# Weight slots, the last expert and the output blocks of a soft mixture of experts

## The chip, the cores and the metric

The program runs on one core of a Trainium2 chip. The metric is the time of one execution on the device, in microseconds; the lower the better. The core has TensorE (PE, with PEld for its weight loads), VectorE (DVE), ScalarE (ACT), GpSimd (POOL) and SyncE (SP), whose queue issues every DMA of this kernel; 16 DMA engines move the data.

## The reference

Attention, a gated MLP and a soft mixture of experts stand in a row; the change is in the last. All is fp32.

```python
x = attention(rmsnorm(q), rmsnorm(k), v)     # 4 batches, 12 heads, 448 tokens, 64 -> [1792, 768]
x = (silu(x @ w_gate) * (x @ w_val)) @ w_out # 768 -> 1536 -> 768
logits = x @ phi                             # [1792, 32]: 8 experts x 4 slots
d = softmax(logits, over tokens)
slot_input = (d.T @ x).reshape(8, 4, 768)
for e in range(8):
    slot_out[e] = relu(slot_input[e] @ w1[e]) @ w2[e]   # 768 -> 1024 -> 768
c = softmax(logits, over slots)
out = c @ slot_out                           # [1792, 768]
```

## The kernel before

Attention pairs of heads and the MLP's weight tiles run interleaved in an order written out by hand; the MLP's last batch ends at about 664 us of the span. The logits and the slot sums are gathered batch by batch; w_out is applied to the 32 slot sums only (`sip`), and so the experts see 32 rows.

The experts' weights (w1 and w2, 8 x 6 MB) come in 32 units of 1.5 MB (`eunits`), each loaded by `load_unit` into a slot of a ring of 15 (`unit_tile`, 12,288 bytes a partition): 11 slots on the right side of SBUF, free early, of which three first hold w_out, and NL = 4 in the pool `tail` on the left, which overlies the tiles of the MLP (raw, wh0, the x tiles, raw3, wh1, hT in this order) and so comes free as these are read for the last time. Unit u goes to slot (u + 3) % 15, and its load is issued behind the matmuls of unit u - 15. Units are (e, i, n): i = 0 is half of w1, by rows; i = 1 half of w2, by rows; i = 2 half of w2, by columns (pieces of 1,536 bytes, four DMAs of 384 KB). Experts 0 to 5 go by i = 0, 0, 1, 1. Experts 6 and 7 first do both halves of w1; then come the column halves n = 0 of both, then n = 1 of both.

For i = 0 the slot inputs `sit` are stationary (32 columns) and the weights move; four matmuls side by side in column groups fill `hacc`. ACT takes the relu, TensorE transposes, DVE puts the expert's four slots into the zeroed `h1m`. For i = 1 and 2 `h1m` is stationary, and all experts add up in one PSUM tile `so` (four column groups of 192 columns of the output).

The combine weights: `combine1` takes the softmax over slots; `combine2` (POOL) spreads a batch over the four row groups, `combine3` transposes it into `ct`, [128, 1792]: the weights of all tokens, once in each row group. Both run behind units 2 to 7, one batch a unit; `ct` has a tile of its own, the spread weights (`c3`) two.

The output: when n = 0 of experts 6 and 7 is done, `slot_out(0)` copies half of `so` to `sos`, and `output(0, i)` runs for 16 blocks of 112 tokens: two matmuls side by side in two row groups (stationary: 32 rows x 112 tokens of `ct`; moving: 192 columns of `sos`), a copy by DVE and one by ACT into a slot that is free again, and a DMA for one or two blocks. Then come the matmuls of the last two units, `slot_out(1)`, and 16 blocks of the other half. SP's queue issues all these DMAs in program order.

Of the kernel before, what the change touches and what calls it, by code (L numbers as in the profile page):

```python
# [21 lines left out]
def attn_moe_softmoe_kernel(  # L22
# [15 lines left out]
    nc = tc.nc  # L38
# [904 lines left out]
        nc.vector.reciprocal(out=cm, in_=cm)  # L943
        nc.vector.tensor_tensor(out=cv_, in0=cv_, in1=cmb, op=ALU.mult)

    def combine2(pool, b):

        c3s[b] = pool.tile([CP, NC, 4, NS], F32, tag="c3", name="c3", bufs=2)
        nc.gpsimd.tensor_copy(out=c3s[b], in_=ce[:, b].unsqueeze(2).to_broadcast([CP, NC, 4, NS]))

    def combine3(b, ct):

        c3 = c3s.pop(b)
        cp = pt_tile("cp")
        for c in range(NC):
            nc.tensor.transpose(
                cp[:, CP * c : CP * c + CP], c3[:, c].rearrange("p i s -> p (i s)"), ident[:CP, :CP]
            )
        nc.scalar.copy(out=ct[:, S * b : S * b + S], in_=cp[:, :S])


    KD2, KH2 = KD // 2, KH // 2


    eunits = [(e, i, n) for e in range(E - 2) for i in range(2) for n in range(2)]
    eunits += [(e, 0, n) for e in (E - 2, E - 1) for n in range(2)]
    eunits += [(e, 2, n) for n in range(2) for e in (E - 2, E - 1)]
    NE = len(eunits)

    NR, NL = (9, 2), 4  # L970
    NRT = sum(NR)
    wtile = {}
    wo = []
# [2 lines left out]
    def unit_tile(u):  # L976

        slot = (u + NG) % (NRT + NL)
        pool = pools[0 if slot < NR[0] else 1 if slot < NRT else 2]
        m = 2 if NRT <= slot < NRT + 2 or slot == NRT + 3 else 1  # L980
        t = [pool.tile([P, KD2 * F // m], F32, tag=f"w{slot}{i}", name="w") for i in range(m)]
        return t[0] if m == 1 else t

    def load_wo(g):
        t = unit_tile(g - NG).rearrange("p (j d) -> p j d", d=DM)
        for j in range(4):
            nc.sync.dma_start(out=t[:, j, :], in_=w32["o", 4 * g + j])
        wo.append(t)

    def load_unit(u):  # L990
        if u >= NE:
            return
        e, i, n = eunits[u]
        if i == 0:

            w, src = F, w1[e, KD2 * P * n : KD2 * P * (n + 1)].rearrange("(m p c) f -> p m (c f)", m=1, p=P)
        elif i == 1:
            w, src = DM, w2[e, KH2 * P * n : KH2 * P * (n + 1)].rearrange("(m p k) f -> p m (k f)", p=P, k=2)
        else:
            w, src = DM // 2, w2[e, :, DM // 2 * n : DM // 2 * (n + 1)].rearrange("(m p k) f -> p m k f", p=P, k=2)  # L1000
        t = unit_tile(u)
        if isinstance(t, list):
            hf = KD2 * F // 2
            wtile[u] = lambda c, o, m: t[(c * w + o) // hf][:, (c * w + o) % hf : (c * w + o) % hf + m]
            for h in range(2):
                nc.sync.dma_start(out=t[h], in_=src[:, h] if i else src[:, 0, hf * h : hf * (h + 1)])
            return
        tv = t.rearrange("p (c f) -> p c f", f=w)
        wtile[u] = lambda c, o, m: tv[:, c, o : o + m]
# [411 lines left out]
    OS = [2, 2]  # L1421
    TF, TO = [0, 0, 0, 0, 0, 0, 0], [0, 16, 16, 16]
    FILL = {7: 2, 9: 1, 1: 2, 15: 2}
    LDO = "w0 v0 w1 w2".split()
    PF = [2, 2]
    ENG = dict(rel0="ap", rel1="aa", top0="p", top1="pp", wl1="vv", wh1="a", hid="a", pvd="avavavaa", pvd1="avvvaaaa", nm="pp", qz="vp", rb="a", xh="a", wpa="aa", wpq="a")
    NPOOL = 2
    ORDA = [
# [105 lines left out]
    with tc.manual_schedule():  # L1534
# [27 lines left out]
        ct = tp_.tile([P, NT], F32, name="ct")  # L1562
        sos = tp_.tile([P, DM // 4], F32, name="sos")
        so = ps.tile([P, 192], F32, tag="g", name="so")
        FQ = F // 4
        DQ = DM // 4
        hacc, h1s = {}, {}
        ot = {}

        def slot_out(n):  # L1570

            r = slice(2 * NS * n, 2 * NS * (n + 1))
            fill(TF[5 + n])
            (nc.scalar.copy if n else nc.vector.tensor_copy)(out=sos[r], in_=so[r, :])

        def output(n, i):
            b, c = divmod(i, NC)
            if b not in ot:
                ot[b] = unit_tile(NE + b).rearrange("p (c d) -> p c d", d=DM)[:CP]
            ob = out[S * b : S * b + S].rearrange("(p c) d -> p c d", c=NC)  # L1580
            cs = slice(384 * n, 384 * n + 384)
            ops = [(s_tile(k) if k < 3 else pt_tile("op"))[:CP, :DQ] for k in ((2 * i + j) % 6 for j in range(2))]
            for j in range(2):
                r = slice(NS * (2 * n + j), NS * (2 * n + j + 1))
                nc.tensor.matmul(  # L1585
                    ops[j], ct[r, S * b + CP * c : S * b + CP * c + CP], sos[r], start=True, stop=True
                )
            for j, eng in enumerate((nc.vector.tensor_copy, nc.scalar.copy)):
                eng(out=ot[b][:, c, DQ * (2 * n + j) : DQ * (2 * n + j + 1)], in_=ops[j])
            m = 1 if b == 0 and c < OS[n] else 2  # L1590
            if m == 1 or c % 2:
                nc.sync.dma_start(out=ob[:, c + 1 - m : c + 1, cs], in_=ot[b][:, c + 1 - m : c + 1, cs])

        for u, (e, i, n) in enumerate(eunits):
            w = wtile.pop(u)
# [29 lines left out]
                        )  # L1625
                    h1s[e] = h1m
            else:
                for kh_ in range(KH2 * n, KH2 * n + KH2) if i == 1 else range(KH):
                    for j in range(4) if i == 1 else (2 * n, 2 * n + 1):
                        nc.tensor.matmul(  # L1630
                            so[NS * j : NS * j + NS, :],
                            h1s[e][:, kh_, :],
                            w(kh_ % KH2, DQ * j, DQ) if i == 1 else w(kh_, DQ * (j - 2 * n), DQ),
                            start=(e == 0 and kh_ == 0),
                            stop=(e == E - 1 and kh_ == KH - 1),
                        )
            if NE - 5 <= u < NE:
                fill(TF[u - NE + 5])
            load_unit(u + NRT + NL)
            if u == 1:  # L1640
                combine1(tp_)
            if 2 <= u < 2 + B:
                combine2(tp_, u - 2)
            if 4 <= u < 4 + B:
                combine3(u - 4, ct)
            if u == NE - 3:
                slot_out(0)
            if u == NE - 1:
                slot_out(1)
            if u >= NE - 3:  # L1650
                for b in range(TO[u - NE + 3], TO[u - NE + 4]):
                    output(0, b)
        for b in range(B * NC):
            output(1, b)
    tp_.release()
    pools[1].release()
    xp_.release()
# [30 lines left out]
```

## Time and profile before

| | |
|---|---|
| median of 3 runs | 774.86 us (774.71 to 779.64) |
| the profiled execution, its own time | 779.46 us |
| its span | 777.5 us |
| mean granted TensorE clock | 0.988 |
| busy: PE, PEld, DVE, ACT, POOL | 732.2, 568.0, 481.3, 395.6, 422.3 us |
| moved by DMA | 157.82 MB, mean 203 GB/s |

The span runs from the first instruction to the last event of the profiled execution; the execution's own time has 1.96 us more. Busy PE is not PE at its peak, since matmuls are pipelined. The page's slices are 19.4 us each.

### The profile page before, as it was taken

To read this page: it belongs to the slowest core of one execution; us is meant where nothing else is said; L and a number is where in the kernel's file an instruction comes from. 1 tells how busy PE (TensorE), PEld (TensorE's weight loads), DVE (VectorE), ACT (ScalarE), POOL (GpSimd) and SP (SyncE) were. 2 spreads that over 40 slices of the span, in tenths; PEclk is the share of its full clock that TensorE was granted. 3 is DMA by queue.
4 is the path that set the end of the run, shared out by engine and by line. 5 is a ranking of instruction groups with operands and counts; after the bars stand their busy time and mean duration, and the time that the engine had idled before them with its cause. 6 is when DMAs were issued, how large, how long until landed. Compare 5 with 4: busy or idle time off the path is not lost.

```text
span 777.5 us, 20265 instructions
## 1 busy us (share of the span) xinstructions
PE 732.2 (94%) x8348; PEld 568.0 (73%) x8348; DVE 481.3 (62%) x938; ACT 395.6 (51%) x857; POOL 422.3 (54%) x367
## 2 busy tenths in 40 slices
PE   6699999999999999999999989999999999888685
PEld 5466667787778778888888778888878888555354
DVE  6889898888888966777676767676242222320023
ACT  5778788887798643554454534444222222210023
POOL 5886884656465665877677567855334444010000
PEclk9999999999999999999999999999999999999988
DMA  7667756755675641544433432344248878899997
GB/s 229 161 207 218 226 165 222 250 175 190 195 258 186 192 122 59 149 146 142 126 95 113 141 109 71 96 130 130 83 146 290 309 264 331 320 418 416 419 371 252
DMA packets 74972, 157.82 MB, mean 203 GB/s; under 512 B 9344, under 2 KB 49280, under 8 KB 73344
## 3 DMA queue, kind: packets, MB, share of 16 engines
q1 hardware_dynamic: 74880, 156.53, 60.3%
q8 instruction: 66, 1.08, 0.6%
q14 instruction: 26, 0.21, 0.1%
HBM read 136.84 MB, written 19.66 MB: 201 GB/s over the span
## 4 chain that ended last, share of the span: by engine, by line
PE 82%; DMA 6%; DVE 5%; ACT 3%; issue 2%; POOL 1%; SPq 0%; ACTq 0%; DVEq 0%; POOLq 0%
PE pg L711 45%; PE s L508 6%; PE xp L645 6%; PE tp L587 4%; PE so L1630 4%; DMA w<-in_moe_w_dram 2%; PE s L1601 2%; PE xp L610 2%; PE tq L439 2%; PE lp L763 2%; PE s L512 2%; PE sp L840 2%; PE s L610 1%; DMA r<-in_moe_w_out_dram 1%; PE s L1585 1%
## 5 line engine op out<-in xcount | busy, mean ns | idle before, releaser
L711 PE MATMUL pg<-xh,wh 128*128 128x448 f32 x576 | 219.0, 380 | 0.0
L711 PE MATMUL pg<-xl,wh 128*128 128x448 f32 x576 | 210.2, 365 | 0.0
L711 PE MATMUL pg<-xh,wl 128*128 128x448 f32 x432 | 157.8, 365 | 0.0
L535 ACT ACTIVATE pr<-s,sm 128x448 f32<-128x448 f32 x168 | 106.3, 637 | 82.7 <-DVE sm L523 78.0
L711 PEld LDWEIGHTS pg<-xh,wh 128*128 128x128 f32 x576 | 108.1, 188 | 24.2 <-issue 15.5
L246 ACT CAST wh<-raw 128x768 fp32r<-128x768 f32 x96 | 79.8, 832 | 71.7 <-PE pg L711 35.1
L711 PEld LDWEIGHTS pg<-xl,wh 128*128 128x128 f32 x576 | 108.4, 188 | 8.6 <-issue 0.6
L254 POOL TENSOR_TENSOR wl<-raw,wh 128x768 fp32r<-128x768 f32 x48 | 88.5, 1846 | 47.6 <-ACT wh L246 47.6
L523 DVE TENSOR_REDUCE sm<-s 128x1 f32<-128x448 f32 x168 | 97.7, 614 | 16.6 <-PE s L512 8.7
L218 POOL TENSOR_TENSOR hpos<-hpos,hneg 128x768 f32<-128x768 f32 x36 | 66.4, 1844 | 51.7 <-ACT hneg L209 35.3
L711 PEld LDWEIGHTS pg<-xh,wl 128*128 128x128 f32 x432 | 81.1, 188 | 6.9
L552 POOL TENSOR_SCALAR pr<-pr,su 128x448 f32<-128x448 f32 x84 | 55.5, 673 | 45.0 <-DVE su L548 42.7
L254 POOL TENSOR_TENSOR raw<-raw,wh 128x768 fp32r<-128x768 f32 x24 | 44.2, 1843 | 50.1 <-ACT wh L246 50.1
L391 POOL TENSOR_TENSOR ri<-ss,mhalf 128x16 f32<-128x16 f32 (+2 forms) x24 | 67.3, 2804 | 2.0
L508 PE MATMUL s<-ka,qa 64*128 64x448 f32 x432 | 63.4, 397 | 1.8 <-DVE ka L65 1.6
L413 POOL TENSOR_TENSOR qn<-qk,ri 128x512 f32<-128x512 f32 (+1 forms) x46 | 58.8, 1282 | 0.7
L631 DVE STREAM_TRANSPOSE pT<-pr 128x448 f32<-128x448 f32 x84 | 50.8, 630 | 7.9 <-POOL pr L552 7.9
L711 PE MATMUL pg<-xh,raw 128*128 128x448 f32 x144 | 53.0, 368 | 0.8 <-POOL raw L254 0.8
L732 DVE SCALAR_TENSOR_TENSOR ht<-ht,pg 128x448 f32<-128x448 f32 x48 | 29.7, 618 | 38.4 <-ACT ht L725 38.1
L587 PE MATMUL tp<-ident,pr 128*112 128x128 f32 x336 | 50.3, 280 | 2.9 <-ACT pr L535 2.2
L508 PEld LDWEIGHTS s<-ka,qa 64*128 64x128 f32 x432 | 34.9, 184 | 22.4 <-issue 13.3
L587 PEld LDWEIGHTS tp<-ident,pr 128*112 128x112 f32 x336 | 37.3, 134 | 17.9 <-issue 4.7
(180 smaller groups left out, 1172.2 us busy)
## 6 DMA issues: line engine op xcount, KB each, us to landing
w<-in_moe_w_dram SPq DMA_DIRECT2D x22, 1536.0 KB, 11.9
raw<-w SPq DMA_DIRECT2D x72, 384.0 KB, 4.9
w<-raw SPq DMA_DIRECT2D x36, 384.0 KB, 3.5
vt<-in_v_dram SPq DMA_DIRECT2D x60, 224.0 KB, 4.0
r<-in_moe_w_out_dram SPq DMA_DIRECT2D x12, 768.0 KB, 5.1
r<-in_moe_w_gate_dram SPq DMA_DIRECT2D x12, 768.0 KB, 5.2
r<-in_moe_w_val_dram SPq DMA_DIRECT2D x12, 768.0 KB, 5.5
w<-in_moe_w_dram SPq DMA_DIRECT2D x12, 768.0 KB, 13.2
```

Source lines behind the costliest of these rows:

```text
L218: eng.tensor_tensor(out=hp, in0=hp, in1=hn, op=ALU.subtract)
L246: (EV[ENG["wh1"]] if u - NO < NU else nc.scalar.copy)(out=wh, in_=wst[u]["raw"])
L254: eng.tensor_tensor(out=wl, in0=wst[u]["raw"], in1=wst[u]["wh"].bitcast(F32), op=ALU.subtract)
L391: nc.gpsimd.tensor_tensor(out=ri, in0=ss, in1=mhalf[:p, : len(ns)], op=ALU.pow)
L413: eng.tensor_tensor(out=st[i]["qn"][:, n].rearrange("p c h d -> p h c d"), in0=st[i]["qk"][: rows(i), n], in1=st[i]["ri"][:, n] .rearrange ...
L508: nc.tensor.matmul(sc[j], qa[r, wt, c * P : (c + 1) * P], ka[r, mv, :], start=(n == 0), stop=(n == 2))
L523: nc.vector.tensor_reduce(out=d["sm"][:, j : j + 1], in_=d["sc"][j], axis=AX.X, op=ALU.max, negate=True)
L535: nc.scalar.activation(out=p, in_=d["sc"][j], func=AF.Exp, bias=d["sm"][:, j : j + 1], accum_out=st[i]["su"][:, c, j : j + 1])
L552: nc.gpsimd.tensor_scalar(out=p, in0=p, scalar1=su[:, j : j + 1], scalar2=1.0, op0=ALU.mult, op1=ALU.mult)
L587: nc.tensor.transpose(tp[:CP, ck * P : (ck + 1) * P], pr[:, ck * CP : (ck + 1) * CP], ident)
L631: nc.vector.transpose(out=pT[:, 6 - c if j else c, :], in_=st[i][c]["pr"].pop(j))
L711: nc.tensor.matmul(d[r], wt[:, P * c : P * c + P], mv, start=(c == 0 and n == 0), stop=(c == KD - 1 and n == 2),)
```

## The change

- The ring has 16 slots (NL = 5). The four tail slots are now cut in 2, 2, 1 and 4 parts, each part a tile and a DMA of its own; the fifth is one tile. `ct` and `c3` give up their tiles: they take a slot of the ring (`ctile`, the one of unit 16) from unit 18 on, and `combine2` and `combine3` move behind units 18 to 23.
- `ct` is now in the order of the tokens (ACT writes every fourth column); `output` picks its tokens from it with a step of 14.
- Experts 0 to 6 all go by i = 0, 0, 1, 1; only expert 7 goes by column halves. Experts 0 to 6 add up in `so`, which DVE copies to `sos`; each half of expert 7 has a PSUM tile `sol`, which DVE adds to its half of `sos`.
- The output has 14 blocks of 128 tokens (token 14 p + c in partition p of block c), in groups of 4, 4, 4 and 2. One step `output(n, g, h)` makes a group's 192 columns h of half n: two matmuls of 96 columns a block, one DVE copy and one ACT copy for the whole group; with h = 1 comes one DMA for the group. Six of the eight steps of half 0 stand between the last unit's matmuls, two behind each of its first three quarters; then come the other two and half 1.

```diff
-    def combine2(pool, b):
-        c3s[b] = pool.tile([CP, NC, 4, NS], F32, tag="c3", name="c3", bufs=2)
+    def ct_():
+        if not ctile:
+            ctile.append(unit_tile(NE))
+        return ctile[0][:, :NT]
+    def combine2(b):
+        ct_()
+        o = NT + 512 * (b % 2)
+        c3s[b] = ctile[0][:CP, o : o + 512].rearrange("p (c i s) -> p c i s", c=NC, i=4)
...
-        nc.scalar.copy(out=ct[:, S * b : S * b + S], in_=cp[:, :S])
+        nc.scalar.copy(
+            out=ct_()[:, S * b : S * b + S].rearrange("q (p c) -> q c p", c=NC),
+            in_=cp[:, :S].rearrange("q (c p) -> q c p", c=NC),
+        )
...
-    eunits = [(e, i, n) for e in range(E - 2) for i in range(2) for n in range(2)]
-    eunits += [(e, 0, n) for e in (E - 2, E - 1) for n in range(2)]
-    eunits += [(e, 2, n) for n in range(2) for e in (E - 2, E - 1)]
+    eunits = [(e, i, n) for e in range(E) for i in (0, 2 if e == E - 1 else 1) for n in range(2)]
-    NR, NL = (9, 2), 4
+    NR, NL = (9, 2), 5
...
-        m = 2 if NRT <= slot < NRT + 2 or slot == NRT + 3 else 1
+        m = {NRT: 2, NRT + 1: 2, NRT + 3: 4}.get(slot, 1)
...
+        def slot_out(n):
+            o = sos[:, DQ * n : DQ * n + DQ]
+            nc.vector.tensor_tensor(out=o, in0=o, in1=sol[n][:, :DQ], op=ALU.add)
+        def output(n, g, h):
+            if g not in ot:
+                ot[g] = unit_tile(NE + 1 + g).rearrange("p (c d) -> p c d", d=DM)
+            m = min(4, NB - 4 * g)
+            ops = [s_tile(k) if k < 3 else pt_tile("op") for k in ((4 * g + 2 * h + j) % 6 for j in range(2))]
+            for c in range(m):
+                for j in range(2):
+                    r = slice(NS * (2 * h + j), NS * (2 * h + j + 1))
+                    nc.tensor.matmul(
+                        ops[j][:, DQ * c : DQ * c + DQ],
+                        ct_()[r, 4 * g + c :: NB],
+                        sos[r, DQ * n : DQ * n + DQ],
+                        start=True,
+                        stop=True,
+                    )
+            for j, eng in enumerate((nc.vector.tensor_copy, nc.scalar.copy)):
+                o = DH * n + DQ * (2 * h + j)
+                eng(
+                    out=ot[g][:, :m, o : o + DQ],
+                    in_=ops[j][:, : DQ * m].rearrange("p (c d) -> p c d", d=DQ),
+                )
+            if h:
+                cs = slice(DH * n, DH * n + DH)
+                nc.sync.dma_start(out=ob[:, 4 * g : 4 * g + m, cs], in_=ot[g][:, :m, cs])
...
+                for k_, kh_ in enumerate(range(KH2 * n, KH2 * n + KH2) if i == 1 else range(KH)):
+                    for j in range(4):
+                        r = slice(NS * j, NS * j + NS)
                         nc.tensor.matmul(
+                            so[r, :] if i == 1 else sol[n][r, :DQ],
                             h1s[e][:, kh_, :],
+                            w(kh_ % KH2 if i == 1 else kh_, DQ * j, DQ, 2 if i == 1 else 1),
...
+                    if i == 2 and n == 1 and k_ in (1, 3, 5):
+                        for _ in range(2):
+                            output(*outs[0].pop(0))
+                if e == E - 2 and i == 1 and n == 1:
+                    nc.vector.tensor_copy(out=sos, in_=so)
...
+            if CB + 2 <= u < CB + 2 + B:
+                combine3(u - CB - 2)
+            if CB <= u < CB + B:
+                combine2(u - CB)
+            if i == 2:
+                slot_out(n)
+        for a in outs[0] + outs[1]:
+            output(*a)
```

Here CB = 18, NB = 14, DH = 384 and DQ = 96 (192 before).

## Rows read from the trace of the kernel before

**Rows 1.** Page, part 2: DMA engines' busy tenths in 40 slices.
```profile
DMA  7667756755675641544433432344248878899997
```
**Rows 2.** Windows: length, busy time of each engine, granted clock, DMA share, GB/s.
```profile
671.00:674.00 3.00, 1.98 (x40) 0.97 (x18) 1.89 (x6) 1.24 (x3) 0.00 (x0) 1.00 0.54 143
677.00:680.00 3.00, 2.89 (x35) 1.37 (x27) 0.00 (x0) 1.16 (x2) 0.00 (x0) 1.00 0.88 302
680.00:740.00 60.00, 47.59 (x784) 28.56 (x784) 5.23 (x21) 5.45 (x12) 4.46 (x11) 0.97 1.01 416
739.00:740.00 1.00, 0.00 (x0) 0.00 (x0) 0.00 (x0) 0.00 (x0) 0.00 (x0) 1.00 1.00 381
740.00:755.00 15.00, 12.65 (x118) 7.72 (x120) 2.40 (x9) 2.07 (x7) 0.00 (x0) 0.77 1.06 371
```
**Rows 3.** Timeline of SP's DMA queue, 663 to 682 us: start, length, what.
```profile
663.73 0.38 SPq L1011 DMA_DIRECT2D w<-in_moe_w_dram  x1
672.14 1.27 SPq L1006 DMA_DIRECT2D w<-in_moe_w_dram  x2
676.82 3.75 SPq L1011 DMA_DIRECT2D w<-in_moe_w_dram  x3
```
**Rows 4.** Chain that ended last: start, length, what.
```profile
686.33 2.81 PE so L1630 x64
...
696.05 0.53 PE cp L956 x4
...
722.61 18.70 DMA w<-in_moe_w_dram
...
744.40 7.75 PE so L1630 x64
...
758.28 5.35 PE so L1630 x64
```
**Rows 5.** Windows of the output; landing of DMAs of 762 to 766 and 771 to 774.
```profile
758.00:763.00 5.00, 5.00 (x64) 3.46 (x62) 0.65 (x2) 0.62 (x2) 0.00 (x0) 1.00 1.03 354
764.00:766.00 2.00, 1.98 (x24) 1.74 (x24) 1.35 (x5) 1.26 (x4) 0.00 (x0) 1.00 0.17 59
766.00:776.00 10.00, 3.72 (x44) 2.73 (x40) 4.04 (x13) 3.85 (x13) 0.00 (x0) 0.86 0.91 272
...
DMA to landing us min/median/max: 2.1/2.1/2.1
...
L1592 SPq DMA_DIRECT2D out_dram<-w x2: 417/1222/2027, 770.6 to 772.7; - x2
...
DMA to landing us min/median/max: 3.9/4.5/5.2
```
**Rows 6.** Copies by DVE: a group by shape, then the first and last of half 1.
```profile
L1574 DVE COPY sos<-so 64x192 f32<-64x192 f32 x1 | 0.3, 350 | 7.4 <-PE so L1630 7.4
...
764.63 0.68 DVE L1589 COPY w<-s 112x192 f32<-112x192 f32 x2 [5.96 <-PE s L1585]
...
769.75 0.36 DVE L1589 COPY w<-s 112x192 f32<-112x192 f32 x1
```
**Rows 7.** TensorE's weight loads: two runs, four groups by shape, one line's.
```profile
118.57 0.97 PEld L288 LDWEIGHTS wpq<-stack,hT 128*128 128x128 f32 x8
679.46 2.17 PEld L1551 LDWEIGHTS sit<-stack,si 128*128 128x128 f32 x12 [0.80 <-ACT si L1544]
...
L439 PEld LDWEIGHTS tq<-ident,qn 128*128 128x128 f32 x48 | 5.2, 140 | 3.1 <-issue 3.0
L288 PEld LDWEIGHTS wpq<-stack,hT 128*128 128x128 f32 x24 | 2.9, 191 | 0.6 <-ACT pT L598 0.3 <-issue 0.3
L1616 PEld LDWEIGHTS htp<-ident,hr 128*128 128x128 f32 x16 | 2.5, 207 | 8.5 <-ACT hr L1613 8.5
L1551 PEld LDWEIGHTS sit<-stack,si 128*128 128x128 f32 x12 | 2.2, 260 | 0.8 <-ACT si L1544 0.8
...
L645 PEld LDWEIGHTS xp<-pT,vt x224: 127/131/132, 274.8 to 283.0; 32*64 32x64 f32 x112
```

More of the change, by code (lines that the diff above doesn't have):

```diff
@@ L944, in combine1, with combine3 @@
         nc.vector.tensor_tensor(out=cv_, in0=cv_, in1=cmb, op=ALU.mult)
-    def combine2(pool, b):
-        c3s[b] = pool.tile([CP, NC, 4, NS], F32, tag="c3", name="c3", bufs=2)
+    ctile = []
+    def ct_():
[6 more added lines that the diff above has]
+        c3s[b] = ctile[0][:CP, o : o + 512].rearrange("p (c i s) -> p c i s", c=NC, i=4)
         nc.gpsimd.tensor_copy(out=c3s[b], in_=ce[:, b].unsqueeze(2).to_broadcast([CP, NC, 4, NS]))
-    def combine3(b, ct):
+    def combine3(b):
         c3 = c3s.pop(b)
@@ L988, in load_wo, with views @@
         wo.append(t)
+    def views(t, o, n, k):
+        if k == 1:
+            return t[:, o : o + n]
+        r, o = o // DM * DM, o % DM
+        return t[:, r : r + DM].rearrange("p (k d) -> p k d", k=k)[:, :, o : o + n]
+    DH = DM // 2
     def load_unit(u):
@@ L1002, in load_unit @@
         if isinstance(t, list):
[L1003 to L1006, printed above, removed]
+            m = len(t)
+            hf = KD2 * F // m
+            wtile[u] = lambda c, o, n, k=1: views(t[(c * w + o) // hf], (c * w + o) % hf, n, k)
+            full = src.rearrange("p m x -> p (m x)") if i == 0 else None
+            for h in range(m):
+                if i == 0:
+                    part = full[:, hf * h : hf * (h + 1)]
+                else:
+                    part = src[:, 2 * h // m, hf * h % (2 * DM) : hf * h % (2 * DM) + hf]
+                nc.sync.dma_start(out=t[h], in_=part)
             return
         tv = t.rearrange("p (c f) -> p c f", f=w)
-        wtile[u] = lambda c, o, m: tv[:, c, o : o + m]
+        wtile[u] = lambda c, o, n, k=1: views(t, c * w + o, n, k)
         if i < 2:
@@ L1420, in attn_moe_softmoe_kernel @@
     LF = 7
-    OS = [2, 2]
-    TF, TO = [0, 0, 0, 0, 0, 0, 0], [0, 16, 16, 16]
     FILL = {7: 2, 9: 1, 1: 2, 15: 2}
@@ L1425, in attn_moe_softmoe_kernel @@
     PF = [2, 2]
+    CB = 18
     ENG = dict(rel0="ap", rel1="aa", top0="p", top1="pp", wl1="vv", wh1="a", hid="a", pvd="avavavaa", pvd1="avvvaaaa", nm="pp", qz="vp", rb="a", xh="a", wpa="aa", wpq="a")
@@ L1561, in attn_moe_softmoe_kernel @@
         warm_tag[0] = "v"
-        ct = tp_.tile([P, NT], F32, name="ct")
-        sos = tp_.tile([P, DM // 4], F32, name="sos")
-        so = ps.tile([P, 192], F32, tag="g", name="so")
+        DQ = DH // 4
+        sos = tp_.tile([P, 2 * DQ], F32, name="sos")
+        so = ps.tile([P, 2 * DQ], F32, tag="g", name="so")
         FQ = F // 4
-        DQ = DM // 4
         hacc, h1s = {}, {}
+        NB = NT // P
+        ob = out.rearrange("(p c) d -> p c d", c=NB)
         ot = {}
+        sol = []
@@ L1570, in slot_out @@
         def slot_out(n):
[L1572 to L1586, printed above, removed]
-                )
[L1588 to L1592, printed above, removed]
@@ L1594, in attn_moe_softmoe_kernel @@
+        outs = [[(n, g, h) for g in range((NB + 3) // 4) for h in range(2)] for n in range(2)]
         for u, (e, i, n) in enumerate(eunits):
@@ L1627, in attn_moe_softmoe_kernel @@
             else:
-                for kh_ in range(KH2 * n, KH2 * n + KH2) if i == 1 else range(KH):
-                    for j in range(4) if i == 1 else (2 * n, 2 * n + 1):
+                if i == 2:
+                    sol.append(ps.tile([P, 512], F32, tag="vg"[n], name="sol"))
+                for k_, kh_ in enumerate(range(KH2 * n, KH2 * n + KH2) if i == 1 else range(KH)):
+                    for j in range(4):
+                        r = slice(NS * j, NS * j + NS)
                         nc.tensor.matmul(
-                            so[NS * j : NS * j + NS, :],
+                            so[r, :] if i == 1 else sol[n][r, :DQ],
                             h1s[e][:, kh_, :],
-                            w(kh_ % KH2, DQ * j, DQ) if i == 1 else w(kh_, DQ * (j - 2 * n), DQ),
-                            start=(e == 0 and kh_ == 0),
-                            stop=(e == E - 1 and kh_ == KH - 1),
-                        )
-            if NE - 5 <= u < NE:
-                fill(TF[u - NE + 5])
+                            w(kh_ % KH2 if i == 1 else kh_, DQ * j, DQ, 2 if i == 1 else 1),
+                            start=(kh_ == 0 and (i == 2 or e == 0)),
+                            stop=(kh_ == KH - 1 and (i == 2 or e == E - 2)),
+                        )
+                    if i == 2 and n == 1 and k_ in (1, 3, 5):
[3 more added lines that the diff above has]
+                    nc.vector.tensor_copy(out=sos, in_=so)
             load_unit(u + NRT + NL)
@@ L1641, in attn_moe_softmoe_kernel @@
                 combine1(tp_)
[L1642 to L1654, printed above, removed]
+            if CB + 2 <= u < CB + 2 + B:
+                combine3(u - CB - 2)
+            if CB <= u < CB + B:
+                combine2(u - CB)
+            if i == 2:
+                slot_out(n)
+        for a in outs[0] + outs[1]:
+            output(*a)
     tp_.release()
```

## The prediction

> **What bounds the kernel now.** I read the slices of the page first [rows 1]: the DMA row climbs to 9 from slice 35 on and stays there almost to the end. The change touches only this end, so everything is read from there.
>
> In the windows [rows 2] DMA is the bound from 680 us on: share 1.01 and 416 GB/s up to 740. Ahead of that lie two holes: 671 to 674 has a share of 0.54 and loses 1.38 us, 677 to 680 has 0.88 and loses 0.36. SP's queue says why [rows 3]: the load of unit 10 goes out at 663.73, the next (unit 11, both halves) only at 672.14, the three into the old w_out slots from 676.82. The chain of waits then has one weight load of 18.7 us, then TensorE's matmuls for the last four units, and the output [rows 4].
>
> The four units that come by column halves move at 371 GB/s against 416 [rows 2]. The last microsecond before 740 has 381, so I put the change of form at 739.5. The 4 x 1.573 = 6.29 MB take 0.5 us at 381 (0.19 MB), 15 us at 371 (5.57 MB), and 1.4 us more for the last 0.53: the last weight byte moves at about 756.4. TensorE sees a load some 1.8 us after its last byte: the unit that ends at 739.5 releases it at 722.61 + 18.70 = 741.31 [rows 4]. Output half 0 (2.75 MB) queues behind the weights and streams at 354 GB/s; then DMA falls to a share of 0.17 for two microseconds, because half 1 waits for the last expert matmuls (758.28 to 763.63) [rows 4, 5]. Half 1 moves at 272 GB/s, to about 776.2 (10 us give 2.72 of its 2.75 MB); the span ends 1.3 later, at 777.5.
>
> **The change, part by part.**
> **Fifth slot and quarters.** By the pool sizes the four tail slots lie over raw, wh0, x, raw3, wh1 and the first 9,216 bytes of hT; the new one takes exactly the other 12,288 bytes of hT. Quarter 0 of slot 14 is wh1, whose last reader is a gate/value matmul; it is free when unit 10 is issued, 663.7 [rows 3]. The other quarters and the new slot lie in hT, which the last slot sums read until unit 11 is issued, 672.1. So 0.39 MB can move into the first hole: 0.39/416 = 0.94 us. Unit 12 then follows unit 11 at once, instead of waiting for 676.82, and fills the second, 0.36. Gain 1.3 us (bounds 0, if something later holds the slot, and 1.7, both holes). Behind 680 no slot helps: DMA is at its limit there with 15 slots. The added DMAs of quarters cost SP some 0.4 us apiece (0.38 for unit 10 [rows 3]), hidden by a queue that holds some 18 us of loads [rows 4].
>
> **Expert 6 by whole rows.** Two units change form: 3.15 MB at 371 is 8.5 us, at 416 it is 7.6: gain 0.9. With both, the last weight byte moves at 756.4 - 1.3 - 0.9 = 754.2.
>
> **Combine weights later.** Four POOL copies, 16 transposes and 4 ACT copies move from units 2 to 7 to units 18 to 23, around the 18.7 us in which TensorE waits for DMA, which hides them; without that cover a batch's transposes take 0.53 [rows 4], 2.1 us for four. The slot lent to them belonged to unit 16, already done. POOL and ACT have nothing queued behind them that a load needs.
>
> **Last expert alone.** Output half 0 needed units 28 and 29 and covered 30 and 31; now it needs 30 and covers 31 only. Back from 754.2: unit 30's last byte moves 4.2 us earlier (1.573 MB at 371) and is seen 1.8 later, 751.8. Its last quarter is 16 matmul instructions, at 64 in 2.81 us [rows 4] 0.7: 752.5. The DVE add takes about the 0.35 of today's copy [rows 6] and 0.1 to start: 752.95. Unit 31's first quarter is seen at 754.2 - 3.2 + 1.8 = 752.8 and takes 0.7: output matmuls start at 753.5. DMA has nothing from 754.2 to the first finished group, and that is new.
>
> **Output matmuls.** This term decides. Today 64 matmuls of 112 tokens and 192 columns (two passes each, 128 instructions) keep pace with VectorE, whose 16 copies of a half, 0.36 us each, run back to back from 764.63 to 770.11, 0.343 a pair of matmuls [rows 6]. The change makes 112 matmuls of 128 tokens and 96 columns, 224 passes, and reads the stationary operand, ct, at every 14th element. Weight loads of 32 x 64 in four row groups start every 8.2/223 = 0.037 us [rows 7], below the 0.055 that 64 columns take at the 0.111 for 128 found next, so row groups load in parallel: with two at work, 112 passes are left in series. A pass costs the longer of its weight load and its moving columns. Weight loads of 128 columns that lie together: 8 in 0.97 us at 0.191 each, (0.97 - 0.19)/7 = 0.111. At every third element: 12 in 2.17 at 0.260, (2.17 - 0.26)/11 = 0.174 [rows 7]. Every 14th is not in the trace; the bounds are 0.111 and 0.25 (the same step once more). I take 0.174, because the rise of the duration is the same for every second element (0.140 to 0.207, in transposes) as for every third (0.191 to 0.260) [rows 7]; it looks flat in the stride. 112 x 0.174 = 19.5 us, against 12.4 at the lower bound. With the other three quarters of unit 31 in between, 2.1, TensorE ends at 753.5 + 19.5 + 2.1 = 775.1. The last add hides under the two steps left over from half 0.
>
> The Trainium skill (SBUF — State Buffer, Door 1: The DMA port swizzle) says that SBUF has 16-byte lines and that an access to a new line pays. The trace agrees that stride costs, 0.174 against 0.111. By that rule every element at 56 bytes is a new line, where at 12 bytes three in four are and together one in four; in proportion a load would take 0.205 and the stage 3.5 us longer.
>
> **Copies and output DMAs.** 32 copies of up to 384 elements take the place of 128 of 192; a DVE copy took 0.36 for 192 [rows 6], so at most 0.72 and 5.1 us for the seven full pairs of a half, below TensorE's 9.7. The last is a small one: 0.36 and 0.1 to start. The last DMA, 384 KB on an almost empty queue: 2.1 us for 168 KB [rows 5] and 0.22 MB more at 300 GB/s, 2.8. Today the last is issued at 772.7 and lands 3.9 later, 0.9 ahead of the end [rows 5]; I keep the 0.9. Sum: 775.1 + 0.45 + 2.8 + 0.9 = 779.25.
>
> **DMA as a floor.** The first group of blocks is done at 753.5 + 2.8 (16 passes), its copies 0.7 later, and bytes flow after about 0.8 (a small DMA's 2.1 less 0.55 for its bytes, halved): 757.8. 5.5 MB at 300 GB/s (bounds 272 and 354, today's halves) are 18.3 us, so 776.1, and 777.4 with the 1.3. That is under 779.25, not by much.
>
> **Clock.** TensorE was granted 0.77 of full speed over 740 to 755 [rows 2], so part of it at the lower level of 1.2 GHz, after it had waited up to 741.31. 64 instructions for so took 7.75 us there and 5.35 later [rows 4]: 2.4 us. After the change TensorE waits as often, and the output stands right behind the waits. Bounds 0 and 2.4; I take the middle, 1.2: 780.45.
>
> The profiled execution took 779.46 us, 1.96 more than its span, 4.6 above the median of 774.86. The change is 780.45 - 777.5 = +3.0 us; on the median **777.8**.
>
> **The rivals.**
> (a) The stride costs nothing for 32 rows. Then TensorE needs 12.4 us, the first group's bytes flow from 756.8, and DMA sets the end: 5.5 MB at 310 GB/s is 17.8, and 1.3: 775.9, 1.6 faster than now, 773.3 on the median (771.1 to 775.7 for 354 to 272 GB/s). For it: larger blocks, and a deep queue delivers 354 today. Against: [rows 7]. The Trainium skill (TensorE: Matmul & The Clock Gate, LDWEIGHTS (loading the stationary operand)) gives columns/1.2 ns whatever the rows, 107 ns here, and no stride; the trace agrees for the contiguous load alone.
> (b) Slower by more than noise: weight load and matmul of one row group don't overlap, so a pass is 0.174 + 0.083, 28.8 us, +9.3: 787.1. (192 columns stream in 0.167, as two column groups share 64 passes in 5.35 [rows 4]; 96 in half.) It decides from 0.174 + (7.7 - 3.0)/112 = 0.216 us a pass on; a stride that costs this in the load alone does the same. Against: today's pair takes 0.343, where serial passes (0.097 for 112 columns, and 0.167) would take 0.53. The same page (The mechanism) has the rule: weight loads overlap running matmuls only in other row groups; today's pace doesn't agree.
> (c) The change doesn't do what it says: something that I placed wrongly holds the new slot until the w_out slots come free. The 1.3 is missing: 779.1.
> (d) All good at once: the contiguous price and output at the 410 GB/s of the loads: 756.8 + 13.4 + 1.3 = 771.5, 768.9 on the median.
>
> **How the numbers follow.** Forecast 0.46 (775.3 to 781.3; a little of it lies above), (a) 0.25, (b) 0.21, (c) 0.03, (d) 0.05. One per cent, 7.7 us, is what I count as a difference (767.1 and 782.6): the three runs lie 0.6% apart. Faster 0.05 (what lies beyond (d)), slower 0.23 ((b) and the upper edge of the forecast), same 0.72. The range takes in (a) to its fast end and reaches (b): 771 to 787.
>
> **What would show it.** Unit 12's load at about 672.5 and a DMA share near 1 from 674; the last weight some 2 us earlier; a DMA hole of some 3 us between it and the first output; weight loads for the output of about 0.26 us, one every 0.09, with VectorE no longer back to back; TensorE's end within 5 us of the span's. I am wrong if those weight loads last 0.19 and DMA stays full (a), if passes of one row group come at 0.22 or more (b), or if TensorE's clock stays full throughout.

## The result and the profile after

After the change the kernel takes 781.59 us (median of 20 runs, 777.84 to 785.51); the kernel before, on the same chip, 777.63 (20 runs). The ratio is 1.0056, with a 95% interval from 1.0037 to 1.0076: by the means of the runs about 4.4 us slower (the medians lie 4.0 apart), under the one per cent that the prediction counts as a difference. The forecast was +3.0 us. That the absolute time lies 3.8 above the forecast is mostly the base: over 20 runs the kernel before has 777.63, not the 774.86 of three.

The profiled execution took 781.67 us. Single executions drift by some us in stages that the change doesn't touch, so I count from the issue of unit 10's load, the first step that both kernels share: 663.73 before [rows 3], 661.48 after. From there the span ends 113.77 us later before and 118.22 after, +4.45, which agrees with the timed difference. A time of after plus 2.25 is its place on the axis of before, which the prediction used (663.73 less 661.48).

The page's DMA slices, the line that answers [rows 1]: the nines now end one slice earlier, and the output shows as a 7 and a 6.

```profile
DMA  6576656756685641555433443225158788999976
```

Windows of after that answer [rows 2]: length, busy time of PE, PEld, DVE, ACT and POOL, granted clock, DMA share, GB/s. Their place is 2.25 us off from that of the same windows of before; the first hole is less deep (0.82 for 0.54), the second is not seen (1.00 for 0.88), the stretch behind them is at the same limit.

```profile
671.00:674.00 3.00, 2.06 (x105) 1.48 (x109) 1.17 (x5) 1.21 (x5) 0.56 (x2) 1.00 0.82 244
677.00:680.00 3.00, 2.44 (x20) 2.23 (x20) 0.36 (x1) 0.74 (x2) 0.00 (x0) 1.00 1.00 418
680.00:740.00 60.00, 45.98 (x814) 28.26 (x814) 5.24 (x21) 7.27 (x12) 4.14 (x10) 1.00 1.02 417
...
752.00:753.00 1.00, 0.95 (x12) 0.93 (x8) 0.01 (x1) 0.00 (x0) 0.00 (x0) 1.00 0.63 216
754.00:755.00 1.00, 1.00 (x16) 1.00 (x12) 0.56 (x1) 0.48 (x1) 0.00 (x0) 1.00 0.00 0
757.00:758.00 1.00, 1.00 (x19) 1.00 (x17) 0.00 (x0) 0.00 (x0) 0.00 (x0) 0.50 1.01 367
763.00:764.00 1.00, 1.00 (x22) 0.64 (x20) 0.56 (x1) 0.48 (x1) 0.00 (x0) 0.50 0.00 0
```

The last four are microseconds from the first output matmuls on: TensorE busy nearly from end to end (0.95 to 1.00), DMA with the last weights (216 GB/s), at nothing, at 367 GB/s, and at nothing again. What the holes are worth is better read from the bytes that DMA moved in the 20 us behind the issue of unit 10, first before (663.73 to 683.73), then after (661.48 to 681.48): 0.39 MB more, which is 0.94 us at 416 GB/s.

```profile
DMA packets 1024, 6.74 MB, mean 337 GB/s; under 512 B 97, under 2 KB 97, under 8 KB 855
DMA packets 1356, 7.13 MB, mean 356 GB/s; under 512 B 138, under 2 KB 138, under 8 KB 1159
```

SP's queue, against [rows 3]: the first of unit 11's four quarters goes out at 661.95, right behind unit 10, the other three from 669.84 on, and unit 12 follows at 671.83 without a wait, where before the queue had to wait for an old w_out slot. (A line merges issues with waits between them.) The output is now eight DMAs.

```profile
661.48 0.38 SPq L1037 DMA_DIRECT2D w<-in_moe_w_dram  x1
661.95 9.84 SPq L1032 DMA_DIRECT2D w<-in_moe_w_dram  x4
671.83 22.30 SPq L1037 DMA_DIRECT2D w<-in_moe_w_dram  x12
...
755.97 19.17 SPq L1627 DMA_DIRECT2D out_dram<-w  x8
```

DMA over 740 to 780, one slice a microsecond: mean busy tenths, and GB/s. After the weights (until 753) there is nothing for three microseconds, and then the output comes in bursts with holes between the groups of blocks.

```profile
DMA  9999999999996100199139802999004999999910
GB/s 406 418 412 407 358 372 379 372 370 370 369 332 216 41 0 0 39 367 366 39 121 375 290 0 100 373 359 347 0 16 166 373 327 373 343 375 359 376 60 0
```

The groups by shape that answer [rows 6, 7], weight loads of the output and VectorE's copies: a load takes 333 ns, and VectorE, back to back before, waits 9.4 us for TensorE.

```profile
L1612 PEld LDWEIGHTS s<-sos,w 32*128 32x128 f32 x120 | 16.3, 333 | 1.5 <-DVE w L1621 1.2 <-DVE sos L1601 0.3
L1621 DVE COPY w<-s 128x384 f32<-128x384 f32 x8 | 4.5, 558 | 9.4 <-PE s L1612 5.4 <-PE op L1612 4.0
```

The timeline of TensorE, loads and matmuls, first at the full clock and then, from about 756.5 on, at half of it (1.2 GHz): in one row group a load starts every 0.24 us (754.57 to 754.81, 760.26 to 760.50) at either level. Only the quarters of unit 31 (sol) get slower, 0.54 to 0.87.

```profile
754.57 0.34 PEld L1612 LDWEIGHTS s<-sos,w 32*128 32x128 f32 x1
754.81 0.34 PEld L1612 LDWEIGHTS s<-sos,w 32*128 32x128 f32 x1
755.25 0.54 PE L1670 MATMUL sol<-w,h1m 128*32 128x96 f32 x16
759.00 0.87 PE L1670 MATMUL sol<-w,h1m 128*32 128x96 f32 x16
760.26 0.34 PEld L1612 LDWEIGHTS s<-sos,w 32*128 32x128 f32 x1
760.50 0.34 PEld L1612 LDWEIGHTS s<-sos,w 32*128 32x128 f32 x1
```

The chain now ends, where [rows 4] ended with so and its copies, with output matmuls up to 774.4 and one copy; the last DMA is issued at 774.8, lands 3.9 later, and 1.0 after that the span ends.

```profile
774.31 0.06 PE op L1612
774.39 0.32 ACT w L1621
```

### The profile page after: what moved, and what is told of

The parts are those of the page before. It is cut to its first block, busy times and chain, and to the rows that moved or that the text cites. A ratio compares the mean times of both kernels' runs of the same rounds, so it can differ in the third digit from the quotient of the medians.

```text
span 779.7 us, 20533 instructions
## 1 busy us (share of the span) xinstructions
PE 736.8 (95%) x8508; PEld 577.5 (74%) x8508; DVE 477.5 (61%) x924; ACT 394.3 (51%) x840; POOL 421.9 (54%) x367
## 4 chain that ended last, share of the span: by engine, by line
PE 83%; DMA 8%; DVE 5%; issue 2%; ACT 1%; POOL 0%; DVEq 0%; ACTq 0%; SPq 0%; POOLq 0%
PE pg L711 44%; PE s L508 7%; DMA w<-in_moe_w_dram 6%; PE xp L645 6%; PE tp L587 4%; PE tq L439 2%; PE xp L610 2%; PE s L610 2%; PE s L1612 2%; PE lp L763 2%; PE s L512 2%; PE sp L840 1%; PE s L1638 1%; PE wpp L267 1%; PE rb L570 1%
## 5 line engine op out<-in xcount | busy, mean ns | idle before, releaser
L508 PEld LDWEIGHTS s<-ka,qa 64*128 64x128 f32 x432 | 35.3, 186 | 21.6 <-issue 13.5
```

What stands on the lines that cost most here:

```text
L508: nc.tensor.matmul(sc[j], qa[r, wt, c * P : (c + 1) * P], ka[r, mv, :], start=(n == 0), stop=(n == 2))
```

## The experiments

The theory: the strided read of ct makes the weight loads of the output dear, TensorE sets the pace of the output, and DMA waits between groups. Rivals: the order of the work (two row groups at a time, the last expert alone), the clock, or the slots. "Landing to end" is from the landing of the last weight DMA to the end of the span; "aligned end" counts from unit 10's issue. The ratio is to the kernel before, on the same chip, with its 95% interval. "Landing to end" and "aligned end" come from one execution each, and they are not the change of time: for e5 the aligned end lies 3.0 us before that of the kernel before, where the ratio gives +0.7 us (-1.5 to +2.9), and for e8 the two are level, where it gives +2.0 (0.1 to 4.0). Where the two differ, the ratio decides. e2, e3 and e12 ran once and have no ratio.

| kernel | ratio | landing to end, us | aligned end, us |
|---|---|---|---|
| before | 1 | 19.4 | 113.77 |
| after | 1.0056 (1.0037 to 1.0076) | 25.6 | 118.22 |
| e1_step1 | 0.9989 (0.9955 to 1.0023) | 19.7 | 112.48 |
| e5_packed | 1.0009 (0.9981 to 1.0037) | 18.5 | 110.74 |
| e4_slots15 | 1.0104 (1.0068 to 1.0140) | 25.9 | 120.08 |
| e7_pair | 1.0110 (1.0070 to 1.0150) | 28.0 | 121.44 |
| e6_packed_pair | 1.0085 (1.0053 to 1.0117) | | 121.07 |
| e8_four | 1.0026 (1.0001 to 1.0052) | | 113.80 |
| e11_fill | 1.0078 (1.0044 to 1.0112) | | 120.82 |
| e13_packed_four_fill | 1.0006 (0.9979 to 1.0034) | | 112.41 |
| e9_pair4_fill | 0.9973 (0.9944 to 1.0002) | | 110.31 |

**The stride, address alone.** Other columns of ct are read, so each block is weighted by other tokens' weights; the instructions and their order stay.

```diff
-                        ct_()[r, 4 * g + c :: NB],
+                        ct_()[r, P * (4 * g + c) : P * (4 * g + c) + P],
```

> The changed kernel with one edit: the output matmuls take 128 neighbouring columns of ct instead of every 14th, so they use the weights of other tokens; nothing else moves. Theory (the strided weight load sets the tail): a pass of two row groups falls to 0.11 to 0.13 us from the 0.19 of the changed kernel, TensorE's output stage from 22 us to about 14, DMA becomes the bound of the output, and the time falls by 5 to 9 us against the changed kernel, to 1 to 4 us below the kernel before. Rival (the last expert alone leaves DMA idle while its output is made; the stride is hidden): less than 1.5 us.

The group by shape, e1:

```profile
L1612 PEld LDWEIGHTS s<-sos,w 32*128 32x128 f32 x120 | 8.7, 205 | 1.2 <-DVE w L1621 0.6 <-DVE sos L1601 0.3
```

The mean load falls from 333 to 205 ns, and landing to end from 25.6 to 19.7 us. The ratio falls by 5.2 us (0.9989 for 1.0056), at the low end of the 5 to 9 expected. One address explains the output stage's loss.

**The stride, the same result.** The ACT copy of combine3 writes token order into a second free slot, and a VectorE copy puts the columns of a block together behind it.

```diff
-            out=ct_()[:, S * b : S * b + S].rearrange("q (p c) -> q c p", c=NC),
+            out=ctn_()[:, S * b : S * b + S].rearrange("q (p c) -> q c p", c=NC),
...
+        nc.vector.tensor_copy(
+            out=ct_().rearrange("q (c p) -> q c p", c=k)[:, :, S // k * b : S // k * b + S // k],
+            in_=ctn_()[:, S * b : S * b + S].rearrange("q (p c) -> q c p", c=k),
+        )
...
-                        ct_()[r, 4 * g + c :: NB],
+                        ct_()[r, P * (4 * g + c) : P * (4 * g + c) + P],
```

> The changed kernel with ct packed by blocks: combine3 writes the batch in token order to a second free slot, and one DVE copy a batch puts it into ct in block order, so that the output matmuls read neighbouring columns and the result is the reference's. Theory: as with neighbouring columns alone, 5 to 9 us below the changed kernel; the four copies lie in the DMA wait and cost nothing. Rival (the stride is only moved): the four DVE copies reading every 14th element take so long that the expert matmuls wait for h1m, and half or more of the gain is lost.

The group by shape, and DMA over 740 to 780 in slices of 1 us, e5:

```profile
L1624 PEld LDWEIGHTS s<-sos,w 32*128 32x128 f32 x120 | 8.0, 186 | 1.0 <-DVE w L1633 0.6
...
DMA  9999999999985109999999999999991000000000
```

TensorE's output runs from 751.7 to 763.9, 12 us, and DMA is full from 755 to its end: DMA is the bound again. By the ratios e5 is 3.6 us below the changed kernel, where 5 to 9 were expected. The kernel ties with the one before: the holes between the groups are gone, the hole ahead of the first stays.

**The size of the stride.** Every 2nd and every 4th element (again other tokens' columns).

```diff
-                        ct_()[r, 4 * g + c :: NB],
+                        ct_()[r, 2 * P * ((4 * g + c) % 7) : 2 * P * ((4 * g + c) % 7) + 2 * P : 2],
```
```diff
-                        ct_()[r, 4 * g + c :: NB],
+                        ct_()[r, 4 * P * ((4 * g + c) % 3) : 4 * P * ((4 * g + c) % 3) + 4 * P : 4],
```

> The changed kernel with every second column of ct in the output matmuls (the weights of other tokens). Weight load by the slope of the prediction, flat in the stride: 0.26 us long; by lines of 16 bytes in proportion (two elements a line): 0.23 us. Output stage of TensorE 13 to 19 us.

> The changed kernel with every fourth column of ct in the output matmuls (the weights of other tokens, some blocks twice). Flat in the stride: 0.26 us a load, as every third. By lines of 16 bytes: one element a line, so the same 0.33 us as every 14th, and an output stage of 22 us.

Weight loads of e2, two of one row group behind one another, and the group by shape:

```profile
759.48 0.19 PEld L1612 LDWEIGHTS s<-sos,w 32*128 32x128 f32 x1
759.60 0.19 PEld L1612 LDWEIGHTS s<-sos,w 32*128 32x128 f32 x1
...
L1612 PEld LDWEIGHTS s<-sos,w 32*128 32x128 f32 x120 | 8.4, 191 | 1.1 <-DVE w L1621 0.6 <-DVE sos L1601 0.3
```

The group by shape of e3:

```profile
L1612 PEld LDWEIGHTS s<-sos,w 32*128 32x128 f32 x120 | 15.7, 321 | 1.5 <-DVE w L1621 1.2 <-DVE sos L1601 0.3
```

Every 2nd element is as good as neighbours: 191 ns, a load every 0.12 us. Every 4th costs nearly all that every 14th does, 321 of 333 ns. One run each: 781.43 us with an aligned end of 111.81 for e2, 787.14 and 119.96 for e3. e2's time is lost ahead of the stage: unit 10 goes out at 667.59, 6.1 us later than in after.

**The clock.** e3 ran at half the clock in its output, e2 at the full one, so the stride had to be told from the clock. e11 adds warm-up matmuls ahead of the output to the changed kernel, e12 to e3.

```diff
-        warm_tag[0] = "v"
+        warm_tag[0] = "s2"
...
+                    if i == 2 and n == 0 and k_ % 2 == 0:
+                        fill(1)
...
+            if i == 0 and u >= NE - 6:
+                fill(6)
```

> The changed kernel with warm-up matmuls in the waits for the last weights (24 of 128 columns behind each of the last two halves of w1 and of the unit before, 4 ahead of each quarter of unit 30), which keep TensorE busy; output as in the changed kernel. Theory (a strided load is bound by SBUF, not by TensorE's clock): even where the clock stays at full speed a load takes 0.333 us and a pass of a row group 0.243; only the matmuls of unit 31's quarters gain, 1 us, and the time stays within 1.5 us of the changed kernel. Rival (the half clock in the output is the loss, the stride only goes with it): loads of 0.19 to 0.26 us and 4 to 6 us less.

> Every fourth column of ct in the output matmuls (weights of other tokens, some blocks twice), with the same warm-up matmuls, since without them the clock was at half speed all through the output and the load, 0.322 us, was the one of neighbouring columns at that clock. By lines of 16 bytes: at full clock still 0.32 or 0.33. If it is the clock alone: 0.19.

Loads of e12 in a row group, the group by shape, and two windows:

```profile
755.70 0.33 PEld L1612 LDWEIGHTS s<-sos,w 32*128 32x128 f32 x1
755.93 0.33 PEld L1612 LDWEIGHTS s<-sos,w 32*128 32x128 f32 x1
...
L1612 PEld LDWEIGHTS s<-sos,w 32*128 32x128 f32 x120 | 15.7, 322 | 1.5 <-DVE w L1621 1.2 <-DVE sos L1601 0.3
...
754.00:756.00 2.00, 2.00 (x27) 2.00 (x28) 0.33 (x1) 0.29 (x1) 0.00 (x0) 1.00 0.07 17
762.00:764.00 2.00, 2.00 (x27) 1.99 (x24) 0.56 (x1) 0.48 (x1) 0.00 (x0) 0.50 1.01 364
```

At granted 1.00 and at 0.50 the same 27 matmuls pass in two microseconds. e11 has 333 ns for every 14th too, but its time (1.0078) tests little, because the warm-up did not keep the clock up: it fell at about 761, some 4 us into the output, as in after (752.07 to 756.5). e12 took 782.47 in its one run. So the clock costs the strided loads nothing. It does cost loads of neighbours: 186 ns in e5 at the full clock, 322 in e6 at half of it.

**The slots.** The fifth slot is taken away again; the quarters stay.

```diff
-    NR, NL = (9, 2), 5
+    NR, NL = (9, 2), 4
```

> The changed kernel with NL = 4: a ring of 15 slots again, quarters and everything else kept. Theory: the fifth slot fills the hole at 677 to 680 only, 0.4 us, and the quarter the other 0.9; so 0.2 to 0.8 us slower than the changed kernel. Rival (a slot more also keeps DMA busy later): 2 us slower or more. Second rival (the slot is worth nothing): no change.

Two windows of e4:

```profile
673.00:677.00 4.00, 4.00 (x114) 2.29 (x117) 0.04 (x1) 0.80 (x3) 0.00 (x0) 0.57 0.61 212
676.00:680.00 4.00, 3.89 (x43) 1.77 (x35) 0.00 (x0) 1.15 (x2) 0.00 (x0) 0.91 0.59 179
```

The last weight lands 1.55 us later than in after, counted from unit 10 (94.2 for 92.65), where 0.2 to 0.8 was expected; the ratio gives 3.7 us (1.0104 for 1.0056), with intervals that overlap. What the quarters bring forward is missing at 676 to 680, where the share is 0.59 (in after 1.00 from 677 to 680). But the 1.55 is not the slot's price alone: in this execution the granted clock was 0.57 from 673 to 677, where TensorE makes the sums (`sip`) that the old w_out slots wait for, and the load into the first of these goes out 14.55 us behind unit 10, in before and after 13.1. So e4 doesn't show what the quarters gain without the slot.

**The last expert alone.** Experts 6 and 7 share the column halves, as before the change.

```diff
+    eunits = [(e, i, n) for e in range(E - 2) for i in range(2) for n in range(2)]
+    eunits += [(e, 0, n) for e in (E - 2, E - 1) for n in range(2)]
+    eunits += [(e, 2, n) for n in range(2) for e in (E - 2, E - 1)]
...
+                    if i == 2 and n == 1 and k_ % 2 and (e == E - 2 or k_ < KH - 1):
+                        output(*outs[0].pop(0))
```

> The changed kernel with the last two experts by column halves together, as in the kernel before (both n = 0, then both n = 1), and the eight steps of output half 0 spread behind the pieces of the last two units; stride kept. Theory (stride sets TensorE's tail, and the cover adds to it): output matmuls start some 4 us earlier against a last weight 0.9 us later, so 3 to 4 us below the changed kernel, about level with the kernel before; DMA still has holes in the output. Rival (lost cover is all of it): level with or below the kernel before by 2 us or more, and DMA full in the output.

The chain of e7, and a window:

```profile
756.21 0.80 PE sol L1672 x16
757.01 2.19 PE s L1614 x16
...
758.00:760.00 2.00, 2.00 (x28) 1.55 (x26) 0.56 (x1) 0.48 (x1) 0.00 (x0) 0.50 0.00 0
```

I had expected it some 3 to 4 us below after; it is as much above (1.011 for 1.0056). The last weight lands 0.8 us later than in after, as priced, but output half 0 gains nothing from its earlier start: single steps of two row groups alternate with quarters of sol, each step takes 2.19 us for its eight passes, and DMA has nothing meanwhile. The clock was 0.50 from 745 to the end; a quarter of sol takes 0.80 us in the chain, 0.47 in that of after at the full clock.

**Both together.** e5's packing with e7's order.

> The changed kernel with ct packed by blocks (neighbouring columns for the output matmuls) and the last two experts by column halves together, as in the kernel before; the steps of output half 0 lie behind the pieces of the last two units. Theory (with the stride gone, what is left is the DMA hole between the last weight and the first output, 2.6 us, less 0.8 for the slower form of expert 6): 1 to 2.5 us below the packed kernel, 3 us below the kernel before, DMA full from the last weight to the end. Rival (eight single steps on TensorE hold up the matmuls of the last units, and half 1 starts late): no gain on the packed kernel.

The chain of e6, its group by shape, and a window:

```profile
756.57 1.96 PE op L1626 x16
758.53 0.80 PE sol L1684 x16
...
L1626 PEld LDWEIGHTS s<-sos,w 32*128 32x128 f32 x120 | 15.8, 322 | 1.7 <-DVE w L1635 1.1 <-issue 0.6
...
754.00:756.00 2.00, 2.00 (x24) 1.83 (x28) 0.20 (x1) 0.15 (x1) 0.00 (x0) 0.50 0.26 94
```

The gain of the packing is gone: 1 to 2.5 us below e5 were expected, and it lies 5.9 above (1.0085 for 1.0009). The clock is 0.50 from 748 to the end, the loads take 322 ns although they lie together, and a single step takes 1.96 us, hardly less than with the stride.

**Four row groups behind one another.** The stride stays; a group of blocks is one step over four row groups instead of two steps of two.

```diff
+            if h == 0:
+                return
-            ops = [s_tile(k) if k < 3 else pt_tile("op") for k in ((4 * g + 2 * h + j) % 6 for j in range(2))]
+            ops = [s_tile(k) if k < 3 else pt_tile("op") for k in ((4 * g + j) % 6 for j in range(4))]
             for c in range(m):
-                for j in range(2):
-                    r = slice(NS * (2 * h + j), NS * (2 * h + j + 1))
+                for j in range(4):
+                    r = slice(NS * j, NS * (j + 1))
```

> The changed kernel with the two steps h = 0 and h = 1 of a group in one: for each block the four matmuls of the four row groups stand behind one another, then two copies by DVE and two by ACT. Stride, instructions and DMAs are the same. Theory (each row group loads its weights by itself, one strided load of 128 columns in 0.243 us, and the order two by two leaves half of the groups idle): a group of four blocks takes 8 x 0.243 = 1.95 us instead of 3.0 to 3.3, TensorE's output stage 15 to 17 us instead of 22, DMA is nearly full behind its hole, and the time falls by 4 to 6 us against the changed kernel, to about level with the kernel before. Rival (strided loads share one path to SBUF, which is full): 0.06 us an instruction stays, no change.

TensorE's weight loads in e8, two columns of blocks, and the group by shape:

```profile
758.79 0.34 PEld L1614 LDWEIGHTS s<-sos,w 32*128 32x128 f32 x1
758.80 0.34 PEld L1614 LDWEIGHTS op<-sos,w 32*128 32x128 f32 x1
758.80 0.34 PEld L1614 LDWEIGHTS s<-sos,w 32*128 32x128 f32 x1
758.80 0.34 PEld L1614 LDWEIGHTS op<-sos,w 32*128 32x128 f32 x1
759.03 0.34 PEld L1614 LDWEIGHTS s<-sos,w 32*128 32x128 f32 x1
...
L1614 PEld LDWEIGHTS s<-sos,w 32*128 32x128 f32 x120 | 14.5, 333 | 2.0 <-DVE w L1623 1.8
```

Four loads start at once, and the next four 0.24 us later: the price is one of a row group, and all four pay it side by side. The load is as dear as in after, and yet TensorE's output takes 19.3 us for 22.3 (15 to 17 expected) and the aligned end is 4.4 us earlier (113.80 for 118.22). All of it is in half 0: half 1 takes 9.2 us for 8.8, since there the steps of after overlap already. The ratio falls by 2.3 us (1.0026 for 1.0056), with intervals that overlap, so a gain in time is likely and not shown.

**All three.** e13 is packed, four row groups, with the warm-up; e9 has the pair order as well (the edits above).

> The packed kernel (ct by blocks), with the four row groups of a block behind one another and the warm-up matmuls; the last expert alone as in the changed kernel. Theory: the output starts at full clock, the first group takes 0.9 us instead of 1.9, the DMA hole behind the last weight shrinks from 2.6 to about 1.5 us, and DMA is full from there: 1 to 3 us below the packed kernel, so 1 to 3 us below the kernel before. Rival (warm-up delays the last weights' matmuls): no gain or a loss of 1 us.

> Packed ct, the four row groups behind one another, warm-up matmuls, and the last two experts by column halves together, so that output half 0 is made while the last two units load. Theory (the pair was slow with packed ct because the clock stayed at half speed from 748 us on, at which neighbouring columns take 0.32 us a load, and because single steps leave half of the row groups idle): with both mended DMA has no hole behind the last weight, and the time is 3 to 6 us below the kernel before, the best of all. Rival (the clock falls in the output all the same): half clock in the row, 0.32 us a load, level with the kernel before or slower.

A window of e13:

```profile
758.00:760.00 2.00, 2.00 (x64) 1.72 (x60) 1.30 (x4) 1.14 (x4) 0.00 (x0) 1.00 1.03 363
```

DMA over 740 to 780 and the group by shape, e9:

```profile
DMA  9999999975999939999999999600000000000000
...
L1628 PEld LDWEIGHTS s<-sos,w 32*128 32x128 f32 x120 | 7.3, 186 | 4.8 <-issue 2.8 <-DVE w L1637 1.8
```

e13 is no better than e5 (1.0006 for 1.0009; 1 to 3 us less were expected): once DMA runs it is full either way, and the hole behind the last weight stays (a share of 0.26 from 753 to 757). e9 has hardly any hole: output half 0 is ready while the last weights land. It is the fastest kernel here, 773.47 us. Its ratio, 0.9973, is 2.1 us below the kernel before, where 3 to 6 were expected, and the interval just reaches 1, so a gain is likely and not shown. Its clock stayed at 1.00 through the output; whether the four row groups or the warm-up kept it there wasn't tried apart.

## Why the prediction came out as it did

Side and mechanism held: TensorE, on strided weight loads, sets the pace of the output, and the kernel is slower by less than 1%. That the size came out so near is in part luck: the price of a load and the number of passes in series were both wrong, in opposite directions. The profiled difference is 4.45 us against 3.0. On the axis of before:

- **Last weight.** Forecast 2.2 us earlier, measured 1.75 (landing 94.4 before, 92.65 after). The slot and the quarters are worth 0.94 (the 0.39 MB above; 1.3 forecast), expert 6 by whole rows 0.8 (e7; 0.9 forecast), and these make up the 1.75. The 1.3 counted 0.94 for the first hole and 0.36 for the second; 0.94 is what both brought.
- **Start of the output.** Forecast 753.5, measured 752.07 + 2.25 = 754.3: 0.8 late, of which 0.45 is the weight above.
- **Output matmuls, the term that decides.** Forecast 21.6 us with unit 31's quarters (19.5 and 2.1), measured 22.3 (752.07 to 774.37; 20.0 and 2.3), +0.7. Two errors offset each other here, which is luck. The first is the price of a load. The step "the rise of the duration is the same for every second element as for every third; it looks flat in the stride" is wrong. Passes in one row group start every 0.111 us for neighbours [rows 7], 0.12 for every 2nd (e2), 0.174 for every 3rd [rows 7], 0.23 for every 4th (e12), 0.243 for every 14th. The 0.25 that stood as the upper bound was nearly the true price, and 112 passes in series at 0.243 would be 27.2 us. The second is "with two at work, 112 passes are left in series": the two steps of a group were taken to follow one another, and they run partly side by side, on four row groups. A group's 16 passes take 3.2 to 3.3 us in half 0 and 2.2 to 2.5 in half 1, where 16 at 0.243 would be 3.9; e8's order brings the same to half 0. In half 1 DMA keeps level with TensorE: 0.79 MB in 2.2 us is 360 GB/s, and DMA is full from 771 on.
- **Tail.** Forecast 4.15 us behind TensorE (0.45, 2.8, 0.9), measured 5.3: the last DMA isn't on an almost empty queue, because its predecessor of 768 KB, issued at 774.0, is still moving, and takes 3.9 where 2.8 was forecast. With the rest the tail is 1.15 longer.
- **Clock.** Forecast 1.2 us on top, measured nothing on top. The clock did fall, to 0.50 from 756.5 to the end, but strided loads take as long at either level. The term was carried over from so's matmuls, whose time goes with the clock. Only the quarters of unit 31 pay as these do: two of the three in the output took 0.87 us for 0.54, 0.66 in all, which stands in the 22.3 above.

0.8 + 0.7 + 1.15 - 1.2 = 1.45, the whole miss. The combine weights were hidden as forecast: their transposes lie at 715.3 to 725.0, where the chain of after waits 24.21 us for weights (from 704.63). The DMA hole ahead of the output was forecast from 754.2 to 757.8, and measured from about 755.3 to 758.3 on that axis (753 to 756 in after).

On the stride, the Trainium skill (SBUF — State Buffer, Door 1: The DMA port swizzle) wants two hits on a 16-byte line for full bandwidth. The trace agrees: every 2nd element (two on a line) is free, every 3rd and 4th pay. An estimate with the Trainium skill's line goes by the lines that a load touches: 0.174 for 96 of them gives 0.232 for 128 and 0.116 for 64, and 0.23 (every 4th) and 0.12 (every 2nd) were measured. My 0.205 drew its line through the load of neighbours too, which is dearer than its lines (32 of them would be 0.058, and it takes 0.111). The same section of the Trainium skill gives "4 fp32" as the stride that is free, and the runs don't agree: at the full clock every 4th took 0.33 us (e12), neighbours 186 ns (e5).

**The rivals.** (a) A free stride: refuted by e1 and e5, where taking it away wins 6 to 7 us of the output stage in the trace and 5.2 and 3.6 us by the ratios. Its DMA-bound end is what e5 shows. Its 12.4 us for TensorE are not: e5's 12 have unit 31's quarters in them (3 x 0.54), because there too the steps overlap. (b) Serial passes: the sign that the prediction gave for it, passes of one row group at 0.22 us or more, did come, with 0.243. Its cause, load and matmul in series, did not: the 0.243 stays at half the clock, where a quarter's matmuls go from 0.54 to 0.87, and with the same matmuls e2's passes start every 0.12. Its time, 787.1, did not come either, because the steps overlap on four row groups. (c) A slot held: no, unit 12 goes out at 671.83 without a wait. (d) needed neighbours and no hole; e9 comes nearest to it.

## What to carry to other kernels

Before a stationary fp32 operand is read with a stride, look up what its load costs: here every 2nd element was as good as neighbours, every 4th and every 14th took twice as long in a row group at the full clock (0.23 and 0.24 us for 0.111). A copy that puts the elements together, made while TensorE waits, was cheaper than 224 dear loads. Where the load is the bound, matmuls of 32 rows are worth putting on all four row groups behind one another: e8 took 3 us from TensorE's output. A gain in one stage has to be followed to the next: freed of the stride, this output became bound by DMA, and only the order that fills the hole behind the last weight (e9) came out below the kernel before, by 2.1 us that its interval doesn't quite show.

## What was not expected of the hardware

A weight load of 32 rows by 128 columns takes 333 ns with a stride of 14 elements at either clock level, while one of neighbours takes 186 at 2.4 GHz and 322 at 1.2 GHz: at half the clock the stride is almost free (in a row group a load every 0.24 us for 0.21 in e6), so a slow clock can hide its price. The granted clock fell to 0.50 in strided and single-step outputs (after, e3, e4, e6, e7, e8, e11, e12) although TensorE was busy all the time by the trace (1.00 in the windows of after), and in e5, e2, e13 and e9 it stayed at 1.00 while output matmuls ran. That is observed only; no run here says why. Output in DMAs of 768 KB moved at 327 to 376 GB/s in the microseconds that it filled, against 272 in half 1 of the kernel before [rows 5]; half 0 of the kernel before had 354 with smaller DMAs, so their size isn't shown to be the cause.
